# Moving the experts' high halves to GpSimd and the sums of inner features to VectorE

## The chip, the cores and the metric

The kernel runs on one core of a Trainium2 chip. A core has five engines that each work through their own instruction queue in order: TensorE (PE, matrix products; PEld is its weight load), VectorE (DVE), ScalarE (ACT), GpSimd (POOL) and SyncE (SP, which here only issues DMAs). An instruction starts when it is at the head of its queue and the semaphores it waits for have been raised. The metric is the device time of one execution in microseconds (us), lower is better.

## The reference

Three stages follow one another, all in float32:

```python
# 1. linear attention, 4 x 8 heads, 576 positions, head size 64, 128 features
q_p, k_p = phi(q), phi(k)                    # exp(+-(x @ w_phi - max|.|))
num, den = q_p @ (k_p^T v), q_p @ sum(k_p)
x = num / (den + 1e-6)                       # -> 2304 tokens x 512
# 2. a dense layer 512 -> 2048 -> 512
h = x @ w_in;  x = (h * clip(h + 3, 0, 6) / 6) @ w_out
# 3. eight experts, all of them for every token, mixed by P
P = exp(x @ w_gate - max), then 8 rounds of row and column scaling
for e in range(8):
    out += P[:, e:e+1] * (np.maximum(x @ w1[e], 0) @ w2[e])   # 512 -> 1024 -> 512
```

## The kernel before, in words

TensorE multiplies operands of the type float32r. To keep float32 accuracy every operand is split into a high half (a rounding to float32r) and a low half (what is left), and each product is three matmuls: high x high, high x low, low x high (`mm3`, lines 79 to 82). So each operand costs an elementwise instruction for its high half (`hi_act` on ACT, line 67, or `hi_pool` on POOL, line 70) and one for its low half (`lo_dve`, line 73, or `lo_pool`, line 76).

The change lies in stage 3, which takes the last 1,500 us or so. The inner features of an expert are done in two halves, so there are 16 *blocks* (expert, half). A block goes over the tokens in three thirds; block and third make a *unit*, 48 in all. Both matrix products of a unit are done with seven sub-products instead of eight (a Winograd scheme), which asks for sums of operands:

- **Weights** (`w1_prep`, `w2_prep`). Per block POOL makes eight sums of weight tiles (`w_add`, line 663) and `keep` makes fourteen operands (tiles `w1o` and `w2o`, seven each, 128x512 per half). A `w1o` or `w2o` buffer can be written only when TensorE has done with the operand that lay in it (8 buffers for 7 operands). The raw weights (`raw`) come by DMA into two buffers that alternate between `w1` and `w2`; a load starts when its buffer is free.
- **Inner features** (`hidden`). A unit has 14 *products* of six 128x384 matmuls (lines 935 and 873), numbered 0 to 13, into the PSUM banks `att`, `h` and `kv`. Their results are added up and cut at zero: `u` tiles by `kept` (ACT, line 890), `plus` (DVE, line 893) and `relu` (ACT, line 896). `add` (line 899) then makes the three sums s3 = c12 - c11, s2 = s3 + c22 and s1 = c12 + c22 in `st` tiles of 128x768 (two buffers); s4 is made by DVE out of PSUM (line 916). High halves into `h` tiles are ACT's (line 902), low halves DVE's (line 905, and line 910 out of PSUM).
- **Outputs** (`outputs`). 21 *steps* of six 128x256 matmuls into the `acc` banks (four banks). After each step DVE adds the result, weighted by P, to the output rows (line 1008; line 1006 for the first expert). The steps of one unit run between the products of the next: one step after a product in the first part of the unit, two in the second. Steps four to six of a unit share one bank, and a step waits until DVE has read what lies in its bank: so step five cannot begin before DVE has added step four.

The order on each engine is made by a scheduler: instructions with the program's order as priority, taken early by a cost table when their engine is thought idle. `later(n, ...)` (line 863) puts an instruction n products further back in the program.

Of the kernel before, what the change touches and what calls it, by code (L numbers as in the profile page):

```python
# [21 lines left out]
def tile_kernel(ctx: ExitStack, tc, q, k, v, w_phi, w_in, w_out, w_gate, w1, w2, out):  # L22
    nc = tc.nc
# [42 lines left out]
    def hi_act(dst, src, scale=1.0):  # L66
        nc.scalar.activation(dst, src, AF.Copy, scale=scale)  # L67

    def hi_pool(dst, src):
        nc.gpsimd.tensor_scalar(dst, src, 1.0, 1.0, op0=ALU.mult, op1=ALU.mult)  # L70
# [4 lines left out]
    def lo_pool(dst, src, hi):  # L75
        nc.gpsimd.tensor_tensor(out=dst, in0=src, in1=f32(hi), op=ALU.subtract)  # L76
# [588 lines left out]

    def keep(pool, tag, key, src):
        t = pool.tile([P, 2] + list(src.shape[1:]), F32R, tag=tag, name=tag, bufs=8)
        hi_act(t[:, 0], src)
        lo_pool(t[:, 1], src, t[:, 0])
        wops[key] = t  # L670


    def w1_prep(b):
        (a11, a12), (a21, a22) = (raw.pop((b, False, r)) for r in range(2))
        s1 = w_add(a21, a22, ALU.add)
        yield
        keep(wp, "w1o", (b, "s1"), s1)
        s2 = w_add(s1, a11, ALU.subtract)
        yield
        keep(wp, "w1o", (b, "a11"), a11)  # L680
        s4 = w_add(a12, s2, ALU.subtract)
        yield
        keep(wp, "w1o", (b, "s4"), s4)
        yield
        keep(wp, "w1o", (b, "s2"), s2)
        s3 = w_add(a11, a21, ALU.subtract)
        yield
        keep(wp, "w1o", (b, "a12"), a12)
        yield
        keep(wp, "w1o", (b, "s3"), s3)  # L690
        yield
        keep(wp, "w1o", (b, "a22"), a22)
        yield
# [183 lines left out]
    def hidden(b, c, n0, got):  # L877
        T, A, X = {}, {}, {}

        def tmp(name, tag, bufs):  # L880
            T[name] = hp_.tile([P, QB, UW], F32, tag=tag, name=tag, bufs=bufs)
            return T[name]
# [13 lines left out]
            nc.scalar.activation(T[name], T[name], AF.Relu)  # L896

        def add(name, x, y, op):
            nc.gpsimd.tensor_tensor(out=tmp(name, "st", 2), in0=T[x], in1=T[y], op=op)  # L899

        def hi(o, name):
            hi_act(opnd(o)[:, 0], T[name])
# [21 lines left out]
        for i, o in enumerate(XOPS):  # L924
            x_ahead(n0 + i + XR)
            x = xring[n0 + i]
            for q in range(QB):
# [23 lines left out]
                elif o == "b21":  # L951
                    plus("c11", q, ps)
                    if last:
                        later(1, lambda: relu("c11"))
                        later(2, lambda: add("s3", "c12", "c11", ALU.subtract))
                        later(2, lambda: hi("A11", "c11"))
                        later(3, lambda: lo("A11", "c11"))
                        later(3, lambda: hi("S3", "s3"))
                        later(4, lambda: lo("S3", "s3"))
                elif o == "t3":  # L960
                    plus("c22", q, ps)
                    if last:
                        later(1, lambda: relu("c22"))
                        later(2, lambda: add("s2", "s3", "c22", ALU.add))
                        later(2, lambda: hi("A22", "c22"))
                        later(3, lambda: hi("S2", "s2"))
                        later(5, lambda: lo("S2", "s2"))
                        later(6, lambda: lo("A22", "c22"))
                else:
                    nc.scalar.activation(opnd("A12")[:, 0, q], ps, AF.Relu)  # L970
                    later(1, lambda q=q, ps=ps: lo_a12(q, ps))
                    later(3, lambda q=q, ps=ps: s4(q, ps))
                    if last:
                        later(4, lambda: add("s1", "c12", "c22", ALU.add))
                        later(4, lambda: hi("S4", "s4"))
                        later(5, lambda: lo("S4", "s4"))
                        later(5, lambda: hi("S1", "s1"))
                        later(6, lambda: lo("S1", "s1"))
# [132 lines left out]
```

## Time and profile before

| what | value |
|---|---|
| median of the runs | 2375.76 us (2374.69 to 2376.83, two runs) |
| the profiled execution | 2381.45 us, span 2379.7 us |
| busy PE | 2178.1 us (92%) |
| busy DVE | 1507.8 us (63%) |
| busy ACT | 1033.9 us (43%) |
| busy POOL | 1010.6 us (42%) |
| TensorE's granted clock, mean | 0.962 of full speed |
| POOL's sums of inner features (line 899) | 144 instructions, 295.0 us |
| ACT's high halves of `w1o` and `w2o` | 224 instructions, 140.9 us |

Busy shares are means over stages with different limits. TensorE's matmuls overlap in the records, so its busy time counts pipelined work, and what it loses is read from the idle time before its instructions and from the time that a block takes.

### The profile page before, as it was taken

The page shows a single profiled execution, that of the slowest core. Times are in us where ns is not written, and L with a number is a line of the kernel's source. Part 1 is how long each engine was busy: PE and PEld are TensorE (multiplying, and loading weights), DVE is VectorE, ACT ScalarE, POOL GpSimd, SP SyncE. Part 2 cuts the span into 40 slices and gives each one's busy share as a digit, 9 for nine tenths or more (in the row PEclk, how much of TensorE's full clock was granted, in tenths as well). Part 3 has the DMA queues.
Part 4 walks back from the last instruction along what each step waited for, and adds up shares of the span by engine and source line. Part 5 has one row for each costly group of instructions (what it writes and reads, how often), then busy time and mean ns, then how long its engine had stood idle before and what let it go on. Part 6 is the DMA issues. An engine that isn't in the chain of part 4 may idle for free.

```text
span 2379.7 us, 35438 instructions
## 1 busy us (share of the span) xinstructions
PE 2178.1 (92%) x13659; PEld 2023.3 (85%) x13659; DVE 1507.8 (63%) x2476; ACT 1033.9 (43%) x1868; POOL 1010.6 (42%) x703
## 2 busy tenths in 40 slices
PE   8898999999997998899988999989899998999998
PEld 6676778887886888798988989889898988989898
DVE  6887565654425467576766666666666666767676
ACT  5666465554324443244433434334343433444342
POOL 2543343331103544554644445454454634546331
PEclk9899999999999999899999999999999999999999
DMA  6587664546627544464645545455454545646454
GB/s 178 189 281 237 186 200 137 176 155 209 221 98 229 186 164 165 144 211 168 212 169 183 199 169 206 168 177 190 173 197 171 203 169 180 211 170 215 169 184 148
DMA packets 207704, 439.95 MB, mean 185 GB/s; under 512 B 72984, under 2 KB 129944, under 8 KB 207536
## 3 DMA queue, kind: packets, MB, share of 16 engines
q1 hardware_dynamic: 207536, 437.69, 55.1%
q8 instruction: 108, 1.77, 0.3%
q14 instruction: 60, 0.49, 0.1%
HBM read 399.51 MB, written 38.12 MB: 184 GB/s over the span
## 4 chain that ended last, share of the span: by engine, by line
PE 57%; POOL 15%; DVE 13%; ACT 6%; issue 4%; DMA 4%; SPq 1%; POOLq 0%; DVEq 0%; ACTq 0%
PE ps_acc L80 9%; PE ps_acc L81 8%; PE ps_acc L82 8%; POOL ws L663 5%; DVE h L73 5%; POOL st L899 5%; PE ps_att L80 4%; PE ps_att L82 4%; PE ps_att L81 4%; PE ps_h L80 4%; PE ps_h L81 3%; PE ps_h L82 3%; ACT h L67 2%; PE ps_kv L80 2%; PE ps_kv L82 2%
## 5 line engine op out<-in xcount | busy, mean ns | idle before, releaser
L80 PE MATMUL ps_acc<-w2o,h 128*128 128x256 f32 x2016 | 583.6, 290 | 130.9 <-DVE acc L1008 116.2
L82 PE MATMUL ps_acc<-w2o,h 128*128 128x256 f32 x2016 | 575.2, 286 | 0.0
L81 PE MATMUL ps_acc<-w2o,h 128*128 128x256 f32 x2016 | 575.0, 285 | 0.0
L1008 DVE SCALAR_TENSOR_TENSOR acc<-ps_acc,pm,acc 128x256 f32<-128x256 f32 x882 | 408.1, 478 | 192.4 <-PE ps_acc L82 185.5
L80 PEld LDWEIGHTS ps_acc<-w2o,h 128*128 128x128 f32 x2016 | 388.9, 193 | 149.7 <-DVE acc L1008 128.0
L81 PEld LDWEIGHTS ps_acc<-w2o,h 128*128 128x128 f32 x2016 | 390.1, 193 | 0.0
L82 PEld LDWEIGHTS ps_acc<-w2o,h 128*128 128x128 f32 x2016 | 389.8, 193 | 0.1
L899 POOL TENSOR_TENSOR st<-u 128x768 f32<-128x768 f32 x96 | 206.2, 2148 | 376.5 <-ACT u L896 307.6
L73 DVE TENSOR_TENSOR h<-st,h 128x768 fp32r<-128x768 f32 x192 | 246.4, 1283 | 108.8 <-ACT h L67 108.6
L67 ACT ACTIVATE h<-st 128x768 fp32r<-128x768 f32 x192 | 162.6, 847 | 323.4 <-POOL st L899 277.0
L896 ACT ACTIVATE u<-u 128x768 f32<-128x768 f32 x144 | 121.8, 846 | 310.1 <-DVE u L893 309.7
L80 PE MATMUL ps_att<-xr,w1o 128*128 128x384 f32 x576 | 202.6, 352 | 8.8 <-DMA xr<-xs_b 5.3
L81 PE MATMUL ps_att<-xr,w1o 128*128 128x384 f32 x576 | 200.7, 348 | 0.0
L82 PE MATMUL ps_att<-xr,w1o 128*128 128x384 f32 x576 | 200.4, 348 | 0.0
L73 DVE TENSOR_TENSOR h<-u,h 128x768 fp32r<-128x768 f32 x96 | 142.6, 1486 | 15.9 <-ACT h L67 15.7
L890 ACT COPY u<-ps_att 128x384 f32<-128x384 f32 x192 | 91.8, 478 | 135.9 <-PE ps_att L82 134.2
L80 PE MATMUL ps_h<-xr,w1o 128*128 128x384 f32 x384 | 131.3, 342 | 4.9 <-DMA xr<-xs_b 3.7
L899 POOL TENSOR_TENSOR st<-st,u 128x768 f32<-128x768 f32 x48 | 88.8, 1850 | 110.8 <-ACT u L896 107.9
L80 PE MATMUL ps_kv<-xr,w1o 128*128 128x384 f32 x384 | 131.4, 342 | 1.3 <-DVE u L893 0.8
L76 POOL TENSOR_TENSOR w2o<-ws,w2o 128x512 fp32r<-128x512 f32 x64 | 83.1, 1300 | 114.3 <-ACT w2o L67 110.2
L81 PE MATMUL ps_h<-xr,w1o 128*128 128x384 f32 x384 | 130.4, 340 | 0.0
L82 PE MATMUL ps_h<-xr,w1o 128*128 128x384 f32 x384 | 130.2, 339 | 0.0
(266 smaller groups left out, 5027.3 us busy)
## 6 DMA issues: line engine op xcount, KB each, us to landing
xr<-xs_t SPq DMA_DIRECT2D x192, 768.0 KB
xr<-xs_b SPq DMA_DIRECT2D x144, 768.0 KB
w<-scratch SPq DMA_DIRECT2D x128, 512.0 KB
raw<-in_moe_w_dram SPq DMA_DIRECT2D x64, 512.0 KB
scratch<-cw SPq DMA_DIRECT2D x32, 512.0 KB
xs_t<-xo SPq DMA_DIRECT2D x36, 256.0 KB
raw<-in_moe_w_in_dram SPq DMA_DIRECT2D x16, 512.0 KB
raw<-in_moe_w_out_dram SPq DMA_DIRECT2D x16, 512.0 KB
```

What stands on the lines that cost most here:

```text
L67: nc.scalar.activation(dst, src, AF.Copy, scale=scale)
L73: nc.vector.tensor_tensor(out=dst, in0=src, in1=f32(hi), op=ALU.subtract)
L76: nc.gpsimd.tensor_tensor(out=dst, in0=src, in1=f32(hi), op=ALU.subtract)
L80: nc.tensor.matmul(o, lhsT=wh, rhs=xh, start=start, stop=False, skip_group_check=chk)
L81: nc.tensor.matmul(o, lhsT=wh, rhs=xl, start=False, stop=False, skip_group_check=chk)
L82: nc.tensor.matmul(o, lhsT=wl, rhs=xh, start=False, stop=stop, skip_group_check=chk)
L663: nc.gpsimd.tensor_tensor(out=t, in0=x, in1=y, op=op)
L890: nc.scalar.copy((tmp(name, "u", 5) if q == 0 else T[name])[:, q], ps)
L896: nc.scalar.activation(T[name], T[name], AF.Relu)
L899: nc.gpsimd.tensor_tensor(out=tmp(name, "st", 2), in0=T[x], in1=T[y], op=op)
L1008: nc.vector.scalar_tensor_tensor(out=a, in0=ps[:, sl], scalar=pm[:, ti, e:e + 1], in1=a, op0=ALU.mult, op1=ALU.add)
```

## The change

Two lines. In `keep` the high half of an expert's weight operand is made by POOL (`hi_pool`) where ACT made it (`hi_act`); POOL already made the low half and the sums. In `add`, inside `hidden`, the sums of inner features s1, s2 and s3 are made by DVE where POOL made them.

```diff
     def keep(pool, tag, key, src):
         t = pool.tile([P, 2] + list(src.shape[1:]), F32R, tag=tag, name=tag, bufs=8)
-        hi_act(t[:, 0], src)
+        hi_pool(t[:, 0], src)
         lo_pool(t[:, 1], src, t[:, 0])
         wops[key] = t
@@ hidden @@
         def add(name, x, y, op):
-            nc.gpsimd.tensor_tensor(out=tmp(name, "st", 2), in0=T[x], in1=T[y], op=op)
+            nc.vector.tensor_tensor(out=tmp(name, "st", 2), in0=T[x], in1=T[y], op=op)
```

So 224 ACT instructions of 128x512 become POOL instructions, and 144 POOL instructions of 128x768 become DVE instructions. The order on the engines moves with them. On DVE, at the end of a unit, from the sum into `u` of product 9 on (`u<-ps_att`; `h<-u` and `h<-st` are low halves, `st<-...` the sums), before:

```order
L893 TENSOR_TENSOR u<-ps_att,u 128x384
L1008 SCALAR_TENSOR_TENSOR acc<-ps_acc,pm,acc 128x256 x2
L73 TENSOR_TENSOR h<-u,h 128x768
L893 TENSOR_TENSOR u<-ps_h,u 128x384
L1008 SCALAR_TENSOR_TENSOR acc<-ps_acc,pm,acc 128x256 x2
L73 TENSOR_TENSOR h<-st,h 128x768
L893 TENSOR_TENSOR u<-ps_kv,u 128x384
L1008 SCALAR_TENSOR_TENSOR acc<-ps_acc,pm,acc 128x256 x2
L910 SCALAR_TENSOR_TENSOR h<-ps_h,h 128x384
```

and now:

```order
L893 TENSOR_TENSOR u<-ps_att,u 128x384
L1008 SCALAR_TENSOR_TENSOR acc<-ps_acc,pm,acc 128x256 x2
L899 TENSOR_TENSOR st<-u 128x768
L893 TENSOR_TENSOR u<-ps_h,u 128x384
L1008 SCALAR_TENSOR_TENSOR acc<-ps_acc,pm,acc 128x256
L73 TENSOR_TENSOR h<-u,h 128x768
L1008 SCALAR_TENSOR_TENSOR acc<-ps_acc,pm,acc 128x256
L893 TENSOR_TENSOR u<-ps_kv,u 128x384
L73 TENSOR_TENSOR h<-st,h 128x768
L1008 SCALAR_TENSOR_TENSOR acc<-ps_acc,pm,acc 128x256 x2
L899 TENSOR_TENSOR st<-st,u 128x768
```

The sums s3 and s2 now stand in DVE's own queue, ahead of the low halves that need them; s1 follows in the same way after the rows shown. On POOL, at the start of a block's second unit, when the next block's `w1` weights have arrived, before:

```order
L663 TENSOR_TENSOR ws<-raw_16576 128x512
L663 TENSOR_TENSOR ws<-ws,raw_16552 128x512
L663 TENSOR_TENSOR ws<-raw_16552,ws 128x512
L76 TENSOR_TENSOR w1o<-ws,w1o 128x512
L663 TENSOR_TENSOR ws<-raw_16552,raw_16576 128x512
L899 TENSOR_TENSOR st<-u 128x768 x2
L899 TENSOR_TENSOR st<-st,u 128x768
```

and now:

```order
L663 TENSOR_TENSOR ws<-raw_15595 128x512
L70 TENSOR_SCALAR w1o<-ws 128x512
L663 TENSOR_TENSOR ws<-ws,raw_15571 128x512
L76 TENSOR_TENSOR w1o<-ws,w1o 128x512
L663 TENSOR_TENSOR ws<-raw_15571,ws 128x512
L663 TENSOR_TENSOR ws<-raw_15571,raw_15595 128x512
L70 TENSOR_SCALAR w1o<-raw_15571 128x512
```

No sum of inner features stands behind the weights' sums any more, and POOL's queue in the middle of stage 3 holds nothing but weights. The order of the matmuls on TensorE within a unit is the same in both kernels.

## Rows read from the trace of the kernel before

**Rows 1.** Busy us (instructions) by stretch: PE, PEld, DVE, ACT, POOL; granted clock; DMA.

```profile
1195.55:1294.77 99.22, 91.36 (x631) 90.48 (x631) 67.19 (x111) 40.02 (x65) 49.43 (x31) 0.96 0.55 189
1096.12:2206.32 1110.20, 1015.16 (x6931) 1005.65 (x6931) 733.18 (x1221) 439.15 (x715) 546.18 (x341) 0.96 0.54 185
```

**Rows 2.** Timeline of PE: start us, duration us, instruction, idle time before it and its releaser.

```profile
1246.77 0.39 PE L80 MATMUL ps_acc<-w2o,h 128*128 128x256 f32 x1 [0.67 <-DVE acc L1008]
...
1258.91 0.39 PE L80 MATMUL ps_acc<-w2o,h 128*128 128x256 f32 x1 [1.34 <-DVE acc L1008]
...
1259.73 0.34 PE L80 MATMUL ps_att<-xr,w1o 128*128 128x384 f32 x1
...
1261.49 0.34 PE L80 MATMUL ps_h<-xr,w1o 128*128 128x384 f32 x1
...
1263.96 0.34 PE L80 MATMUL ps_kv<-xr,w1o 128*128 128x384 f32 x1
...
1294.77 0.58 PE L80 MATMUL ps_acc<-w2o,h 128*128 128x256 f32 x1 [5.85 <-DVE acc L1008]
...
1296.21 0.52 PE L80 MATMUL ps_att<-xr,w1o 128*128 128x384 f32 x1
...
1666.37 0.38 PE L80 MATMUL ps_acc<-w2o,h 128*128 128x256 f32 x1 [3.30 <-DVE acc L1008]
```

**Rows 3.** Chain of waits, in order of time: start us, us, engine, tile, line.

```profile
1281.69 1.97 POOL ws L663
...
1290.30 1.77 POOL st L899
1292.09 0.85 ACT h L67
...
1293.84 0.88 DVE acc L1008 x2
```

**Rows 4.** Timeline of DVE at the starts of two units.

```profile
1251.85 0.55 DVE L916 SCALAR_TENSOR_TENSOR st<-ps_kv,st 128x384 f32<-128x384 f32 x1
1252.31 1.98 DVE L73 TENSOR_TENSOR h<-u,h 128x768 fp32r<-128x768 f32 x1
1254.22 0.47 DVE L1008 SCALAR_TENSOR_TENSOR acc<-ps_acc,pm,acc 128x256 f32<-128x256 f32 x1
1254.61 2.20 DVE L73 TENSOR_TENSOR h<-st,h 128x768 fp32r<-128x768 f32 x1
1256.74 0.47 DVE L1008 SCALAR_TENSOR_TENSOR acc<-ps_acc,pm,acc 128x256 f32<-128x256 f32 x1
1257.13 0.94 DVE L73 TENSOR_TENSOR h<-st,h 128x768 fp32r<-128x768 f32 x1
1258.00 0.86 DVE L1008 SCALAR_TENSOR_TENSOR acc<-ps_acc,pm,acc 128x256 f32<-128x256 f32 x2
...
1292.97 0.96 DVE L73 TENSOR_TENSOR h<-st,h 128x768 fp32r<-128x768 f32 x1 [3.39 <-ACT h L67]
```

**Rows 5.** Timeline of POOL at the first of these two places.

```profile
1252.19 1.29 POOL L663 TENSOR_TENSOR ws<-raw,raw 128x512 f32<-128x512 f32 x1
1253.43 2.57 POOL L899 TENSOR_TENSOR st<-u 128x768 f32<-128x768 f32 x1
```

**Rows 6.** Groups by line: busy us, mean ns of one, idle before and its releasers.

```profile
L73 DVE TENSOR_TENSOR h<-st,h 128x768 fp32r<-128x768 f32 x192 | 246.4, 1283 | 108.8 <-ACT h L67 108.6
L73 DVE TENSOR_TENSOR h<-u,h 128x768 fp32r<-128x768 f32 x96 | 142.6, 1486 | 15.9 <-ACT h L67 15.7
```

**Rows 7.** Two lines on POOL: count, duration ns least/median/most, first and last start, shapes.

```profile
L70 POOL TENSOR_SCALAR Eh<-E x24: 611/1045/1552, 243.5 to 527.6; 128x1024 fp32r<-128x1024 f32 x16, 64x512 fp32r<-64x512 f32 x8
L1049 POOL TENSOR_SCALAR acc<-acc,pm x18: 687/697/1425, 962.6 to 991.2; 128x512 f32<-128x512 f32 x18
```

## The prediction

> **What bounds the kernel now.** I read the table of busy time first (TensorE 92%), then the experts' stage alone, since the change touches nothing else that is large. From one long stall of TensorE to the next lies one block; one such block took 99.22 us, eleven took 1110.20 us, 100.93 on average [rows 1]. How long would a block take if TensorE never waited? Between two products with one step between them lie 1.76 us (1259.73 to 1261.49), with two steps 2.47 us (1261.49 to 1263.96) [rows 2]. So a step is 0.71 us and a product 1.05 us; a unit is 14 x 1.05 + 21 x 0.71 = 29.6 us, a block **88.8 us**. Some 10 to 12 us per block are lost, and the timeline shows where: every block has three waits for DVE's reading of the output banks, here 0.67, 1.34 and 5.85 us; the middle one is longer in some blocks (3.30) [rows 2]. They sum to 7.86. The other 2.5 us of this block (99.22 - 88.8 - 7.86) are mostly what follows the long wait: the 128x384 matmul takes 0.52 us instead of 0.34 [rows 2], the lower of the two levels (1.2 instead of 2.4 GHz), for some microseconds; the mean granted clock is 0.96 [rows 1].
>
> Why is DVE late? The chain of waits names POOL: weight sums from 1281.69 on, behind them in its queue the sum of inner features (1290.30), then ACT's high half, then DVE, which idled 3.39 us for it, then two output sums and only then TensorE [rows 3, 4]. So a sum of 1.8 us reaches TensorE as 5.85 us because it stands in the queue behind work that nobody needs yet. The 1.34 us stall has another cause. DVE does not idle there: its low halves, 0.94 us elsewhere, take 1.98 and 2.20 [rows 4]. Beside them POOL's second sum takes 2.57 us [rows 5], 1.77 elsewhere [rows 3]. The first low half starts at 1252.31 and ends 0.81 us after the POOL instruction of 1252.19 to 1253.48; the POOL sum then ends 1.7 us after DVE's; DVE's next ends 0.81 us after POOL's. The two take turns.
>
> **The change, part by part.**
>
> *ACT loses 224 copies.* They cost TensorE nothing by themselves (ACT is under half busy [rows 1]), so I gain nothing here. In return ACT's queue no longer waits for weight buffers.
>
> *DVE gains three sums per unit.* Operands and shape are those of the low halves, so 0.94 us, and 0.87 from start to start [rows 4]. Is there room? The tight stretch of a unit begins when product 9 is done and ends when step five of the next unit wants its bank. For TensorE that is: from 10 x 1.05 + 12 x 0.71 = 19.0 us to 29.6 + 5 x 1.05 + 4 x 0.71 = 37.7 us, 18.7 us. DVE's work in it, counted in the new order: 9 instructions with two SBUF inputs (six low halves, three sums) x 0.87 = 7.8; 13 output sums x 0.40 (1256.74 to 1257.13) = 5.2; 7 that read PSUM x 0.47 (1251.85 to 1252.31) = 3.3 [rows 4]. Together 16.3 us, 2.4 to spare; I take 2.0, since s3 waits some tenths for ACT's cut at zero. Before the change it was 13.7.
>
> *DVE no longer waits for POOL through ACT.* The 5.85 us stall loses its cause whole: no sum on the way to an output stands in POOL's queue now.
>
> *POOL loses 295.0 us and gains 224 high halves.* A 128x512 instruction with one tensor input took 0.61 at the least on another line (64x512, so the same row length) and 0.69 on the nearest [rows 7]: I take 0.65, or 146 us. Per block POOL then works 14 x 0.65 + 22 x 1.29 (low halves and weight sums [rows 5]) = 37.5 us of about 96, before 49.4 of 99.2 [rows 1]. Are weights late? An operand is made when TensorE has left its buffer and is used about a unit (30 us) later, an operand takes 0.65 + 1.29 us, and products follow one another by 3.5 to 5 us per operand: hidden. If that cover went, each late operand would cost its 1.94 us.
>
> *The lock moves.* This is the price that decides. In the trace 288 low halves took 389.0 us, 1.35 each [rows 6], 0.41 more than undisturbed, with POOL busy 50%. POOL's work in the three tight stretches of a block, counted from the new order: at the end of the block 11.6 us (four operands, three sums), at the end of its first unit 11.0 us, at the end of its second 3.9 us. That is 62%, 59% and 21% of 18.7. By proportion a two-input instruction waits 0.41 x 0.61/0.50 = 0.50 us in the first two and 0.17 in the third: 9 x 0.50 = **4.5 us** there, 1.5 us in the third. The bounds are 0.41 (what the trace has on average) and 0.65 (half of 1.29, each meeting a POOL instruction midway); 0.50 is nearer to the measured mean.
>
> The Trainium skill, page "SBUF — State Buffer", section "Who interferes with whom", states this as a rule: a DVE instruction with two SBUF inputs and a GpSimd instruction that reads SBUF exclude one another for a whole instruction, while ACT has ports of its own. The turns above agree. The rule speaks against both halves of this change: the copies leave an engine that locks nobody out, and the sums join those that are locked out. By it alone, with every sum meeting a POOL instruction, the third rival below would come out.
>
> *Sum.* With 2.0 to spare, the first two stretches stall TensorE for 4.5 - 2.0 = 2.5 us each, the third not at all. The lower clock followed stalls of 3.30 and 5.85 us (0.52 at 1296.21), not the one of 1.34 (0.34 at 1259.73) [rows 2]. At 2.5 I count it for one of two stalls, 2.5 us. Block: 88.8 + 5.0 + 2.5 = **96.3 us**, 4.6 less than 100.93. Twelve such blocks give 55 us. The first expert, before 1096, has similar stalls with other partners; 5 us, bounds 0 and 12. The profiled execution took 2381.45 us, 5.7 above the median of 2375.76, so 2381.45 - 60 - 5.7 = **2316 us**.
>
> **The rivals.**
>
> *The stalls only change their name (no change).* Every two-input instruction waits 0.65: 5.9 - 2.0 = 3.9 us in two stretches, the lower clock after both: 88.8 + 7.8 + 5.0 = 101.6 us, 0.7 more than now, 12 x 0.7 - 5 = 3 us: **2379 us**. For it: low halves of 1.98 and 2.20 [rows 4] happen just where POOL has a backlog, as it has in both stretches. Against it: the POOL sums of 1.8 to 2.6 us that locked longest are gone, and high halves hold for 0.65 only.
>
> *The lock costs little.* At 0.41 per instruction 3.7 - 2.0 = 1.7 us, too short for the lower clock: 88.8 + 3.4 = 92.2 us, 12 x 8.7 + 5 = 109: **2267 us**. For it: POOL is busy less in all, and 1.34 us cost no clock. Against it: POOL's work gathers in the tight stretches.
>
> *DVE becomes the bound (slower).* If all three stretches stall and drop the clock, a block is 88.8 + 3s + 7.5; it passes 100.93 from s = 1.5, a wait of 3.5 us per stretch or 0.39 per instruction in all three. At 0.50 everywhere: 88.8 + 7.5 + 7.5 = 103.8, 12 x 2.9 = 35: **2411 us**. At 0.65: 108.0, 85 us more. For it: DVE's spare time falls from 5.0 to 2.4 us. Against it: the third stretch has 3.9 us of POOL work.
>
> *The weights come late,* so that TensorE waits for POOL where it waited for DVE. One operand late by 1.94 us per block: 2316 + 12 x 1.94 = **2339 us**. Against it: a unit of margin, as above.
>
> **How the numbers follow.** The forecast 0.42 (by itself 2294 to 2336: blocks of 94.5 to 98), the unchanged case 0.27, the cheap lock 0.20, slower 0.08, late weights 0.03. Two per cent is 47.5 us, about what a measurement of this kernel can tell from no change: below 2328 it is faster. Of the forecast four fifths lie there (0.33), with the cheap lock 0.53. The rest of the forecast, the unchanged case, late weights and most of the slower case (up to 2423) are within 2%: 0.43. Slower 0.04. The range must hold 0.8: from 2262, which takes in the cheap lock, to 2380, which takes in the unchanged case; the slower case and tails are left out.
>
> **What would show it.** The wait of DVE for ACT's high half (3.39 us) is gone; line 899 is on DVE at 0.94 us undisturbed and 1.2 to 1.4 on average; stalls of TensorE stand only before step five, two per block, 2 to 3 us; blocks of 94 to 98 us; granted clock 0.97 or more; POOL's high halves 0.6 to 0.7 us. It is wrong if step five stalls in all three units, if a stall over 4 us is left, or if TensorE waits for POOL.

## The result and the profile after

The changed kernel took **2309.66 us** (median of 2306.70 and 2312.63), 0.972 of the time before [0.967, 0.978]. Four more runs beside seven of the kernel before gave 2306.24 us and a ratio of 0.970 [0.967, 0.973]. It is faster by about 70 us. The forecast was 2316 us, and the range held it. The blocks came out close to the forecast, in part because errors of its terms cancelled; the first expert gained five times what the forecast had for it, as the traces show. Of all the runs below one, of 5284.61 us with the high halves alone (its others took 2397.49 to 2398.80), was slow and stands in no ratio.

The profiled execution took 2306.70 us, its span is 2304.9. From the page, busy time by engine and the shares of the chain of work that ended last:

```profile
PE 2168.7 (94%) x13659; PEld 2013.9 (87%) x13659; DVE 1634.4 (71%) x2620; ACT 920.9 (40%) x1644; POOL 926.6 (40%) x783
...
PE 61%; DVE 28%; POOL 3%; DMA 3%; issue 2%; ACT 1%; SPq 1%; POOLq 0%; DVEq 0%; ACTq 0%
```

DVE works 126.6 us more and has 28% of the chain; before, POOL had 15% and DVE 13%. The groups by line that answer to [rows 6] and [rows 7] (busy us, mean ns of one | idle us before and its releasers):

```profile
L73 DVE TENSOR_TENSOR h<-st,h 128x768 fp32r<-128x768 f32 x192 | 233.5, 1216 | 4.9 <-ACT h L67 4.9
L73 DVE TENSOR_TENSOR h<-u,h 128x768 fp32r<-128x768 f32 x96 | 117.2, 1221 | 0.1
L899 DVE TENSOR_TENSOR st<-u 128x768 f32<-128x768 f32 x96 | 117.3, 1222 | 0.9 <-ACT u L896 0.9
L899 DVE TENSOR_TENSOR st<-st,u 128x768 f32<-128x768 f32 x48 | 73.9, 1540 | 2.0 <-ACT u L896 1.9
L70 POOL TENSOR_SCALAR w1o<-ws 128x512 fp32r<-128x512 f32 x64 | 42.6, 666 | 79.4 <-PE ps_att L82 60.6 <-PE ps_kv L82 12.5 <-PE ps_h L82 4.9
```

DVE's wait for ACT's high half has gone from 108.6 to 4.9 us. A high half out of a `ws` tile takes 0.67 us on POOL, all 224 together take 172.3 us, 0.77 each. The 432 two-input instructions of DVE took 541.9 us, 1.25 each: 0.31 above the undisturbed 0.94.

TensorE's timeline, which answers to [rows 2] (start us, duration, instruction, idle time before it and its releaser):

```profile
1100.71 0.39 PE L80 MATMUL ps_acc<-w2o,h 128*128 128x256 f32 x1 [0.21 <-DVE acc L1008]
...
1133.24 0.39 PE L80 MATMUL ps_acc<-w2o,h 128*128 128x256 f32 x1 [2.53 <-DVE acc L1008]
...
1166.98 0.38 PE L80 MATMUL ps_acc<-w2o,h 128*128 128x256 f32 x1 [2.33 <-DVE acc L1008]
...
1231.13 0.39 PE L80 MATMUL ps_acc<-w2o,h 128*128 128x256 f32 x1 [2.53 <-DVE acc L1008]
```

The 5.85 us stall is gone. Now each block has two stalls before step five, one where the next block's first unit begins (1133.24; I call this place A) and one at its second unit (1166.98; place B). At its third (place C) only 0.21 us is left. One row of the view of waits sums them from 1035 to 2195 us (engine, tile and line, what it waited for: us in total, times, longest). Before, it was 97.1 us in 35 waits, the longest 5.9:

```profile
PE ps_acc L80 <- DVE acc L1008: 59.7, 36, 2.7
```

Eleven blocks, one of them, and 5 us behind four of the stalls (us, busy PE, PEld, DVE, ACT, POOL with counts; granted clock; DMA), as in [rows 1]:

```profile
1035.44:2102.26 1066.82, 1011.97 (x6931) 1000.27 (x6931) 835.20 (x1320) 361.06 (x561) 485.11 (x396) 0.97 0.55 193
1133.24:1231.13 97.89, 92.82 (x631) 91.77 (x631) 76.04 (x120) 32.80 (x51) 43.80 (x36) 0.97 0.55 191
1133.24:1138.24 5.00, 5.00 (x24) 5.00 (x25) 0.97 (x2) 0.48 (x1) 0.69 (x2) 0.66 0.48 165
1231.13:1236.13 5.00, 5.00 (x36) 5.00 (x37) 2.01 (x4) 0.48 (x1) 1.92 (x2) 1.00 0.64 231
1457.42:1462.42 5.00, 5.00 (x24) 5.00 (x24) 0.97 (x2) 0.48 (x1) 0.00 (x0) 0.66 0.24 64
2005.97:2010.97 5.00, 5.00 (x36) 5.00 (x37) 2.00 (x4) 0.48 (x1) 1.92 (x2) 1.00 0.63 223
```

The mean block is 1066.82 / 11 = 96.98 us. At 1.00 TensorE starts 36 matmuls in 5 us, at 0.66 only 24: a third of 5 us, some 1.7 us, is lost to the lower level (1.2 GHz) each time the clock falls.

### The profile page after: what moved, and what is told of

Read it like the earlier page. It is cut to its first block, busy times and chain, and to the rows that moved or that the text cites. A ratio compares the mean times of both kernels' runs of the same rounds, so it can differ in the third digit from the quotient of the medians.

```text
span 2304.9 us, 35273 instructions
## 1 busy us (share of the span) xinstructions
PE 2168.7 (94%) x13659; PEld 2013.9 (87%) x13659; DVE 1634.4 (71%) x2620; ACT 920.9 (40%) x1644; POOL 926.6 (40%) x783
## 4 chain that ended last, share of the span: by engine, by line
PE 61%; DVE 28%; POOL 3%; DMA 3%; issue 2%; ACT 1%; SPq 1%; POOLq 0%; DVEq 0%; ACTq 0%
PE ps_acc L80 10%; DVE h L73 9%; PE ps_acc L82 9%; PE ps_acc L81 9%; DVE acc L1008 6%; DVE st L899 6%; PE ps_att L80 4%; PE ps_att L81 4%; PE ps_att L82 4%; PE ps_h L80 4%; PE ps_h L81 4%; PE ps_h L82 4%; PE ps_kv L80 2%; PE ps_kv L81 2%; PE ps_kv L82 2%
## 5 line engine op out<-in xcount | busy, mean ns | idle before, releaser
L1008 DVE SCALAR_TENSOR_TENSOR acc<-ps_acc,pm,acc 128x256 f32<-128x256 f32 x882 | 418.5, 478 | 195.1 <-PE ps_acc L82 186.5
L73 DVE TENSOR_TENSOR h<-st,h 128x768 fp32r<-128x768 f32 x192 | 233.5, 1216 | 4.9 <-ACT h L67 4.9
L70 POOL TENSOR_SCALAR w1o<-raw 128x512 fp32r<-128x512 f32 x48 | 42.7, 890 | 431.0 <-PE ps_att L82 399.8
L80 PE MATMUL ps_kv<-xr,w1o 128*128 128x384 f32 x384 | 129.6, 338 | 0.0
L81 PE MATMUL ps_kv<-xr,w1o 128*128 128x384 f32 x384 | 129.1, 336 | 0.0
L82 PE MATMUL ps_kv<-xr,w1o 128*128 128x384 f32 x384 | 128.9, 336 | 0.0
L80 PEld LDWEIGHTS ps_att<-xr,w1o 128*128 128x128 f32 x576 | 112.7, 196 | 10.0 <-DMA xr<-xs_t 4.7
```

The lines of the kernel that those rows point to most:

```text
L73: nc.vector.tensor_tensor(out=dst, in0=src, in1=f32(hi), op=ALU.subtract)
L80: nc.tensor.matmul(o, lhsT=wh, rhs=xh, start=start, stop=False, skip_group_check=chk)
L81: nc.tensor.matmul(o, lhsT=wh, rhs=xl, start=False, stop=False, skip_group_check=chk)
L82: nc.tensor.matmul(o, lhsT=wl, rhs=xh, start=False, stop=stop, skip_group_check=chk)
L1008: nc.vector.scalar_tensor_tensor(out=a, in0=ps[:, sl], scalar=pm[:, ti, e:e + 1], in1=a, op0=ALU.mult, op1=ALU.add)
```

## The experiments

Each kernel ran beside the kernel before on the same chip; times are compared by their ratio to it. Kernels with one run have no interval, and the kernel before itself ranged from 2374.5 to 2382.9 us in one set of seven.

**The sums alone** (from the changed kernel, ACT makes the weights' high halves again):

```diff
-        hi_pool(t[:, 0], src)
+        hi_act(t[:, 0], src)
```

> Half of the change: DVE makes the sums of inner features, ACT goes on making the weights' high halves. Theory (the sums left POOL's queue, and what is left is the lock between DVE and POOL): the whole gain comes from this half, and more of it, since POOL works 28.4 instead of 37.5 us per block. Lock waits in the two busy stretches fall in proportion, stalls before step five from 2.5 and 2.3 us to about 1.3 each, blocks 92 to 95 us, time 2250 to 2295 us. Rival (the copies had to leave ACT, whose queue waits for weight buffers and holds up the cuts at zero): stalls stay at 3 us or more, time 2320 to 2370 us.

Measured: 2257.90 us, ratio 0.948 [0.946, 0.950]. The time is in the range expected, the stalls are not those expected. This half is better than the whole change by some 50 us. TensorE's timeline at places A and B, and the clock over twelve blocks:

```profile
1132.52 0.39 PE L80 MATMUL ps_acc<-w2o,h 128*128 128x256 f32 x1 [0.22 <-DVE acc L1008]
...
1164.65 0.38 PE L80 MATMUL ps_acc<-w2o,h 128*128 128x256 f32 x1 [2.26 <-DVE acc L1008]
```

```profile
1072.82:2177.00 1104.18, 1072.35 (x7543) 1064.72 (x7544) 873.08 (x1437) 488.77 (x776) 386.71 (x259) 1.00 0.59 201
```

The stalls did not shrink alike. The one at A fell from 2.53 to 0.22, the one at B stayed. Why? POOL's and DVE's timelines before the stall at A show it, first of the changed kernel (POOL, then DVE):

```profile
1126.17 1.29 POOL L663 TENSOR_TENSOR ws<-raw,raw 128x512 f32<-128x512 f32 x1
1128.00 0.75 POOL L70 TENSOR_SCALAR w2o<-raw 128x512 fp32r<-128x512 f32 x1 [0.54 <-PE ps_acc L82]
1128.84 1.88 POOL L76 TENSOR_TENSOR w2o<-raw,w2o 128x512 fp32r<-128x512 f32 x1
```

```profile
1128.20 1.36 DVE L899 TENSOR_TENSOR st<-u 128x768 f32<-128x768 f32 x1
1129.48 0.47 DVE L1008 SCALAR_TENSOR_TENSOR acc<-ps_acc,pm,acc 128x256 f32<-128x256 f32 x1
1129.88 1.65 DVE L73 TENSOR_TENSOR h<-st,h 128x768 fp32r<-128x768 f32 x1
```

then of the sums alone:

```profile
1126.58 1.29 POOL L663 TENSOR_TENSOR ws<-raw,raw 128x512 f32<-128x512 f32 x1
1131.40 1.81 POOL L76 TENSOR_TENSOR w2o<-raw,w2o 128x512 fp32r<-128x512 f32 x1 [3.54 <-ACT w2o L67]
```

```profile
1128.61 0.94 DVE L899 TENSOR_TENSOR st<-u 128x768 f32<-128x768 f32 x1
1129.48 0.47 DVE L1008 SCALAR_TENSOR_TENSOR acc<-ps_acc,pm,acc 128x256 f32<-128x256 f32 x1
1129.87 0.94 DVE L73 TENSOR_TENSOR h<-st,h 128x768 fp32r<-128x768 f32 x1
```

In the changed kernel POOL's copy and the low half behind it meet DVE's sum and low half, which take 1.36 and 1.65 us. With the copy on ACT, POOL waits 3.54 us for it, and meanwhile DVE's two instructions run at 0.94. Added up over twelve blocks of each kernel, a two-input instruction of DVE waited 0.47 us at A in the changed kernel and 0.24 with the sums alone, at B 0.45 and 0.44. So the copy costs twice: by its own 0.75 us and by letting the low half into the tight stretch. That is read from the timelines; no run holds the low half back without moving the copy. At B the row of waits in POOL's queue is another: weight sums that wait for a load, the same in both kernels, and the stall is the same. With one stall of 2.1 to 2.5 us per block the mean clock is 1.00 as rounded. It fell after 2 of the 12 stalls (1256.58 and 1812.19), so for example:

```profile
1256.58:1261.58 5.00, 5.00 (x24) 5.00 (x25) 0.97 (x2) 0.48 (x1) 0.00 (x0) 0.69 0.05 12
```

**The high halves alone** (the kernel before, `hi_act` in `keep` replaced by `hi_pool`):

> The other half alone: POOL makes the weights' high halves too, and goes on making the sums of inner features. Theory: the sums stand behind longer weight work in POOL's queue, so the long stall of 5.9 us per block grows by one to two high halves (0.65 us each) or more; blocks of 101 to 106 us, time 2380 to 2440 us. Rival (relief of ACT is worth something by itself): 2320 to 2360 us.

Measured: 2398.70 us, ratio 1.007 [1.005, 1.009]: slower, if by less than 2%. TensorE's timeline:

```profile
1151.88 0.39 PE L80 MATMUL ps_acc<-w2o,h 128*128 128x256 f32 x1 [1.32 <-DVE acc L1008]
...
1199.57 0.58 PE L80 MATMUL ps_acc<-w2o,h 128*128 128x256 f32 x1 [5.34 <-DVE acc L1008]
```

The time is in the range expected, but not by the step expected: the long stall (5.85 before) did not grow, and the smallest one doubled, from 0.67 to 1.32. A block took 102.08 us on average (1099.80 to 2120.58, ten blocks), where it was 100.77. So the two halves pull in opposite ways: the sums gain some 120 us, the high halves cost some 17 alone and some 50 beside the sums.

**No weight work in the steady part** (from the changed kernel; from the third block on nothing is prepared and the second block's operands are used again, so the output is that of other weights):

```diff
     def keep(pool, tag, key, src):
+        if key[0] > 1:
+            wops[key] = wops[1, key[1]]
+            return
```

> The changed kernel without POOL's weight work from the third block on: later blocks use the second block's operands again (raw weights are still loaded; the output is that of other weights). DVE's order and work are unchanged. Theory (lock): every two-input instruction of DVE takes 0.94 us there, no stall before step five, blocks of 89 to 90 us, time 2200 to 2225 us. Rival (DVE's own work and waits fill the tight stretch, POOL or not): stalls of 1.5 us or more stay in every unit, time above 2270 us.

Measured: 2194.06 us (one run), a little under the range expected. The largest group by line of DVE's low halves, and a window over nearly eleven blocks:

```profile
L73 DVE TENSOR_TENSOR h<-st,h 128x768 fp32r<-128x768 f32 x192 | 184.8, 963 | 5.0 <-ACT h L67 4.9
```

```profile
1035.00:2000.00 965.00, 965.00 (x6848) 965.00 (x6847) 733.23 (x1305) 364.24 (x557) 0.00 (x0) 1.00 0.56 188
```

In this run DVE's low halves take 0.97 us on average and the sums 0.98, TensorE does not wait in this window, in which POOL is silent, and 631 matmuls, a block's worth of records, take 965 x 631 / 6848 = 88.9 us: the 88.8 us of the prediction. All that the changed kernel loses per block above this comes with POOL's weight work.

**Each high half written twice** (from the changed kernel, a second `hi_pool(t[:, 0], src)` behind `lo_pool`):

> The changed kernel with each weight high half made twice on POOL (the same values written again): 14 more POOL instructions of about 0.65 us per block. Theory (lock): about 1 us more lock wait in each busy stretch and 0.5 us in the third, stalls of 3.5, 3.3 and 0.5 to 1 us, the lower clock after most of them, blocks about 100 us, time 2335 to 2360 us. Rival (instructions as short as the high halves hardly lock DVE out): stalls as without it, time 2300 to 2315 us.

Measured: 2305.62 us (one run): no slower, a miss. The waits of TensorE from 1035 to 2195 us, and in the whole span a wait of SP's queue for POOL (86.4 us in the changed kernel):

```profile
PE ps_h L80 <- DMA xr<-xs_t: 41.4, 11, 4.8
PE ps_acc L80 <- DVE acc L1009: 15.9, 12, 1.5
```

```profile
SPq L654 <- POOL w1o L70: 141.9, 30, 7.3
```

SP's queue ahead of one of TensorE's waits for a load, and that wait:

```profile
1124.05 0.38 SPq L654 DMA_DIRECT2D raw<-in_moe_w_dram  x1
...
1131.39 0.38 SPq L658 DMA_DIRECT2D raw<-in_moe_w_dram  x1
1131.87 0.46 SPq L733 DMA_DIRECT2D xr<-xs_t  x1
```

```profile
1138.05 0.66 PE L80 MATMUL ps_h<-xr,w1o 128*128 128x384 f32 x1 [4.49 <-DMA xr<-xs_t]
```

The second copy reads the raw weights last and so holds their buffer longer. The next load into it goes out at 1124.05, where it was 1121.34 in the changed kernel. POOL's sums of what it brings come later too, and the load that waits for these sums goes out at 1131.39, where it was 1127.49. Right behind it in SP's queue stands the load of the tokens' operand `xr` (1131.87). TensorE then waits for `xr` in place of DVE, 41.4 us in 11 waits, and for DVE only 15.9 us; that DVE catches up in these pauses is how I read it. The run does not tell what more of the lock costs; it shows that the amount of POOL's work alone does not set the stalls, and that a late reader of the raw weights has a price of its own.

**POOL busy at place C, reading** (from the changed kernel; six sums of 128x768 whose result nobody uses, at the end of each block's second unit):

```diff
+        def load_pool(name):
+            if c == 1:
+                j = hp_.tile([P, QB, UW], F32, tag="junk", name="junk")
+                for _ in range(3):
+                    nc.gpsimd.tensor_tensor(out=j, in0=T[name], in1=T[name], op=ALU.add)
...
+                        later(2, lambda: load_pool("c12"))
...
+                        later(2, lambda: load_pool("c22"))
```

> The changed kernel with POOL kept busy in the third tight stretch of every block, where it has little work: six sums of 128x768 out of the u tiles into a scratch tile that nobody reads, some 11 us, tied to that place by the u tiles they read. DVE's order is the same. Theory (DVE's two-input instructions and POOL's reading ones exclude one another): the third stretch, which stalled 0.2 us, gets a wait of about 0.6 us per two-input instruction and stalls 3 us or more like the other two; the lower clock follows; blocks 101 to 103 us, time 2350 to 2385 us. Rival (the stalls of the first two stretches come from the weights' DMAs, buffers or ACT, and go with them by chance): the third stretch stays at 0.2 us, time 2300 to 2315 us.

**The same place, writing only** (the three sums replaced by one of eight columns and nine fills):

```diff
+                nc.gpsimd.tensor_tensor(out=j[:, 0, 0:8], in0=T[name][:, 0, 0:8], in1=T[name][:, 0, 0:8], op=ALU.add)
+                for _ in range(9):
+                    nc.gpsimd.memset(j, 0.0)
```

> The same with POOL's extra work made of 18 memsets of 128x768 (and two sums of 8 columns that tie them to the place): POOL is busy there but does not read SBUF. Theory (the Trainium skill, page SBUF - State Buffer, section Who interferes with whom: a two-input DVE instruction contends with a GpSimd instruction that reads SBUF, not with one that only writes it): the third stretch stays at 0.2 to 0.5 us, time 2300 to 2320 us. Rival (any POOL instruction locks DVE out): a stall of 2 us or more there, time 2340 us or more.

Measured: 2354.03 us for the reads, 2300.76 us for the writes (one run each). Reads, TensorE's timeline at C and A, and the added work:

```profile
1109.44 0.39 PE L80 MATMUL ps_acc<-w2o,h 128*128 128x256 f32 x1 [2.15 <-DVE acc L1016]
...
1143.58 0.39 PE L80 MATMUL ps_acc<-w2o,h 128*128 128x256 f32 x1 [2.56 <-DVE acc L1016]
```

```profile
L908 POOL TENSOR_TENSOR junk<-u 128x768 f32<-128x768 f32 x96 | 151.5, 1578 | 291.0 <-ACT u L896 286.0
```

Writes, the added work and the waits of TensorE for DVE:

```profile
L909 POOL MEMSET junk<- 128x768 f32 x288 | 213.4, 741 | 16.6
```

```profile
PE ps_acc L80 <- DVE acc L1017: 58.1, 25, 2.7
```

With the reads place C stalls too, 2.15 where it was 0.21 (I had expected somewhat more there; the time is in the range expected); A and B are as they were, 2.56 and 2.42. With the writes, although they are more work (213.4 us against 151.5), the waits stay at 58.1 us (59.7 in the changed kernel), and DVE's 432 instructions at 1.24 us. At C such an instruction waited 0.15 us in the changed kernel, 0.42 with the reads and 0.08 with the writes (by DVE's timeline, over eleven blocks or more). Could the reads have held the `u` tiles too long instead? No instruction waits for the added sums; it is DVE's own instructions that grew, from 541.9 to 578.6 us. So it is POOL's reading that delays DVE, not its being busy. The Trainium skill, page "SBUF — State Buffer", section "Who interferes with whom", states just this: a DVE instruction with two SBUF inputs contends with a GpSimd instruction that reads SBUF, not with one that only writes it. The two runs agree with it.

**Time where DVE is late.** The steps of a unit ran three times the first kind, three times the second, and so on. Alternating the first two kinds by row tile gives DVE more time before the bank is needed again:

```diff
-        for o, h, where, dst in STEPS:
-            for i in range(UP):
+        todo = [(s, i) for i in range(UP) for s in STEPS[:2]] + [(s, i) for s in STEPS[2:] for i in range(UP)]
+        for (o, h, where, dst), i in todo:
```

On the changed kernel:

> The changed kernel with another order of the output steps: the three P1 and three P2 steps of a unit alternate (P1, P2 for each of the three row tiles) where three P1 were followed by three P2. The P2 steps, which share a bank, then have a product and a step between them. Theory (DVE is only late by as much as the lock adds, and it shows at step five because that step has one product, 1.05 us, of slack): the deadline moves back by a product and a step, 1.76 us, so stalls of 2.5, 2.3 and 0.2 become 0.8, 0.6 and 0, the clock stays up, blocks 90 to 91.5 us, time 2220 to 2245 us. Rival (DVE has too much work in a unit, whatever the deadline): the stalls come back at other steps, time 2285 to 2310 us.

With the sums alone (copies on ACT):

> The sums on DVE, the high halves on ACT (as in the run of that half alone), and the alternating order of the P1 and P2 steps. Theory: of its stalls of 0.3 and 2.3 us per block 0 and 0.5 are left, the clock stays up, blocks 89 to 90 us, time 2205 to 2225 us. Rival (DVE's work in the unit): 2245 us or more.

On the kernel before:

> The kernel before with the alternating order of the P1 and P2 steps alone. Theory: the 5.9 us stall, caused by a sum in POOL's queue, shrinks by the 1.76 us of later deadline to about 4.1 and still drops the clock; the stalls of 1.3 to 3.3 us become 0 to 1.5; blocks 95.5 to 97.5 us, time 2310 to 2340 us. Rival (the place of the shared bank is most of the loss): stalls gone, time below 2270 us.

Beside these three the changed kernel ran again:

> The changed kernel again, beside the next three on one chip, to have them against one another: 2300 to 2315 us, ratio 0.970 to 0.975.

Measured: on the changed kernel 2241.90 us, 0.942 [0.940, 0.944]; with the sums alone **2236.79 us, 0.940 [0.939, 0.942]**, the best of those with the right output, though its interval overlaps the one before it; on the kernel before 2318.12 us, 0.975 [0.973, 0.976]; the changed kernel 2306.24 us. The waits of TensorE for DVE from 1035 to 2195 us, in the order of the first three:

```profile
PE ps_acc L80 <- DVE acc L1008: 19.0, 22, 1.1
```

```profile
PE ps_acc L80 <- DVE acc L1008: 17.8, 12, 1.5
```

```profile
PE ps_acc L80 <- DVE acc L1008: 37.2, 52, 1.4
PE ps_att L80 <- ACT u L890: 12.6, 12, 1.1
PE ps_acc L80 <- ACT h L970: 10.3, 12, 0.9
```

On the changed kernel this did what was expected. With the sums alone one stall of about 1.5 us per block is left where 0.5 was expected, so the run missed its forecast by 12 us. On the kernel before the time came out as expected, but not the rows: the one long stall of 4.1 us that I expected is several of about 1 us, some on ACT. A block took 96.24 us there (1138.36 to 1234.60) at a granted clock of 1.00, with 5.4 us of waits, where [rows 1, 2] had 7.86 and a lowered clock: dividing the long stall saved the clock as well.

## Why the prediction was right, and where its sizes were off

**The sums leave POOL's queue.** Right: the 5.85 us stall and DVE's wait of 108.6 us for ACT's high half are gone. Done alone, this gives 0.948.

**ACT loses the copies.** I gained nothing for it, and nothing came: ACT falls by 113 us busy, and with this half alone TensorE's waits for DVE were 104.6 us where they had been 97.1. What I had not seen is that the copy on ACT did something useful: beside the sums on DVE it kept POOL's low half out of the end of the stretch at place A, as I read the timelines.

**The lock moves.** The mechanism holds, by the runs with reads and with writes, and by the one without weight work. So do the places and the stalls: 2.53 and 2.33 us at A and B against 2.5, 0.21 at C against 0. The terms behind them hold too. Over twelve blocks (1035.44 to 2197.22) a two-input instruction waited 0.47 us at A, 0.45 at B and 0.15 at C, by DVE's timeline, where I had 0.50, 0.50 and 0.17; the 0.31 of all 432 is lower because it takes in the parts before and after these blocks. At A that is 9 x 0.47 = 4.2 us, so a stall of 2.53 leaves 1.7 us to spare, where I took 2.0: two small errors in opposite directions. POOL's side was too small. I priced its instructions undisturbed, but a high half took 0.77 us on average instead of 0.65, a low half of the weights (line 76, 329.0 us for 224) 1.47 instead of 1.29, and POOL worked 485.11 / 11 = 44.1 us per block instead of 37.5: the two engines delay each other.

**The clock.** I counted one drop for two stalls. Of the 23 stalls of 2.19 to 2.70 us that stand in the trace after 1035 us, 17 are followed by 5 us at a granted clock of 0.66 to 0.69, 6 by 1.00. So there are 1.5 per block, but each costs 1.7 us and not 2.5: the term is 2.5 us per block, as predicted, by two errors that cancel. That was luck. The row at 1666.37 [rows 2], from which I took that a stall of 3.30 us lowers the clock, does not show it (0.38 us is the duration at full clock), but it was so: the 5 us behind it ran at 0.66.

**The block.** 88.8 + 2.53 + 2.33 + 0.21 + 2.5 = 96.4 us; measured 96.98, predicted 96.3. Between the first and the last stall at place A lie twelve blocks: 1161.78 us (1035.44 to 2197.22), before 1209.23 (1060.25 to 2269.48). The steady part gave 47.45 us where I had 55. A block before took 100.77 us over these twelve, not 100.93 [rows 1], and one after 96.8.

**The first expert** was mis-sized. I gave it 5 us, at most 12. The stall that ends it came at 1060.25 us before and comes at 1035.44 now: 24.8 us. Before, POOL and TensorE in this stretch:

```profile
991.19 0.69 POOL L1049 TENSOR_SCALAR acc<-acc,pm 128x512 f32<-128x512 f32 x1
991.85 1.79 POOL L899 TENSOR_TENSOR st<-u 128x768 f32<-128x768 f32 x1
```

```profile
996.35 0.58 PE L80 MATMUL ps_acc<-w2o,h 128*128 128x256 f32 x1 [7.45 <-DVE acc L1008]
```

POOL also scales the output rows here, 18 instructions [rows 7], and the sums of inner features stood behind them. From 865 to 1000 us the waits over 0.5 us summed to 24.7 us before and to 11.5 after, the longest of these now on a load:

```profile
966.50 0.66 PE L80 MATMUL ps_h<-xr,w1o 128*128 128x384 f32 x1 [5.77 <-DMA xr<-xs_b]
```

The windows of this part, before (first) and after, give most of the rest to the clock, 0.93 against 0.97; estimated from these means that is 14 us lost before and 5 after, and some 3 of the 24.8 us stay unassigned:

```profile
860.00:1060.25 200.25, 173.04 (x1137) 169.60 (x1135) 136.65 (x270) 74.03 (x124) 103.16 (x74) 0.93 0.49 171
```

```profile
860.00:1035.44 175.44, 161.12 (x1108) 158.99 (x1106) 142.32 (x281) 59.00 (x93) 88.56 (x77) 0.97 0.52 186
```

The sums alone also save 19.7 us here (their stall at 1040.58), the high halves alone lose 2.8. I had those 18 rows among mine, for the price of one instruction, and did not ask what stood behind them in the queue.

**The sum.** The span is then shorter by 24.8 + 47.45 + 2.5 behind the last stall = 74.8 us (2379.7 to 2304.9), against 60. The profiled execution after was the faster of its two; by the medians the gain is 66.1 us, against 60 predicted.

**The rivals.** Waits of 0.65 per instruction, which would have left the time unchanged, did not come (0.47 and 0.45), nor did the cheap lock's stalls of 1.7 us and full clock. The slower case needed a stall in all three places; the run with the added reads made one, and its block took 101.73 us (1109.44 to 1211.17), close to the 100.93 from which the prediction let it decide. Late weights did not come: TensorE has no wait for POOL in the steady part.

What stays open is why some stalls of equal length lower the clock and others do not, and some 0.5 us per block that no row of waits holds.

## What to carry to other kernels

Before moving work between engines, look at what stands in front of it in its present queue and at what it will keep out of the way there: here the gain came from a 1.8 us sum that waited behind work that nobody needed yet, and the copies were better left on a half-idle engine, where they cost nothing and kept POOL waiting at a time when it would have been in DVE's way. Do each half of a change alone, since the sums were worth 0.948 and the whole only 0.970. Where a reader is late by a microsecond or two, another order of the steps that use its result can give more than taking work away, here 2306 to 2242 us.

## What the runs showed of the hardware

A stall's length did not decide the clock. After 2.68 us (2005.97) it stayed at 1.00, after 2.19 us (1457.42) it fell to 0.66. With one such stall per block, in the kernel with the sums alone, it fell after 2 of 12, and with two per block, in the changed kernel, after 17 of 23. POOL's fills of 128x768, 0.74 us each and 288 of them, cost DVE nothing that shows, while 96 sums of the same shape brought a stall of 2.15 us to every block.
